# A routed attention kernel whose token lists get slots of 64 B instead of 4 B

## The chip, the core and the metric

The kernel runs on one core of a Trainium2 chip. The metric is the time of the core on the device in microseconds (us): the whole program, from the loads of the inputs to the last row of the output. A profiled execution gives the trace from which the rows below are read.

## What is computed

Three layers follow each other: attention with a window and a few global positions, a layer of eight experts of which each token takes one, and a gated layer.

```python
# attention: batch 4, 8 heads, 768 positions, 64 wide; 8 global positions, window 96
scores = scale * q @ k^T + bias;  scores = where(keep, scores, -1e9)
a = softmax(scores);  attn = a @ v            # x = attn as [3072 tokens, 512]

# experts: 8 experts, 512 -> 1024 -> 512; each token goes to its best one
expert_idx = argmax(x @ w_gate);  gate_w = softmax(...)[expert_idx]
for e in range(8):
    mask = expert_idx == e
    out[mask] = gate_w[mask] * (relu(x[mask] @ w1[e]) @ w2[e])

# gated layer: 512 -> 1536 -> 512
y = (sigmoid(x @ w_gate) * (x @ w_val)) @ w_out
```

## The kernel before

**Attention** (0 to about 225 us) works through 24 tiles of 128 tokens. The order of its steps on each engine is written by a planner in the program (`plan`, with tables of costs and ranks), ahead of any run; on the chip each engine takes its steps in that order and waits where a semaphore is missing. Loads of q, k and v (`load`, L460 and L468) are issued from SyncE's queue (SP) two tiles ahead. The first rows of a sequence's v are copied to a tile `spec` (L617, from ScalarE's queue), and VectorE copies `spec` into later v tiles (L487).

**Routing.** For each tile, the chain of steps X to SC finds each token's expert and its slot in that expert's list: L gives the logits, POS counts with two matmuls how many earlier tokens took the same expert, SI adds this to the start of the expert's region, RR stores the token rows (with the gate weight as column 513) into the DRAM tensor `xd` (L731, SP), and SC (L734, GpSimd, called POOL in the trace) scatters the 128 token ids of the tile into the list `lst` in DRAM. `lst` has a region of 3072 slots for each of the eight experts; the slots of an expert are filled in the order of the tokens. The first scatter waits for the fill of `lst` with the number of an empty row (`clear(0)`, L176, SP), which also fills `ids`.

**Experts** (about 225 to 540 us). `ITEMS` names nine pieces of work, (rank of the expert by load, first slot, number of tokens). For each item `iload` (L970, SP) reads the ids of its slots from `lst` into a tile `idx`, one word into each partition, `gather` (L1015, GpSimd) fetches the token rows of `xd` by `idx`, `xgate`, `xturn`, `xhigh` and `xlow` prepare them, and `mm1` (L1100) and `mm2` (L1117) multiply. `icopy` (L1087, SP) copies the item's part of `lst` behind the others into `ids`, so that `ids` holds all tokens in the order of the expert work. The first item's expert is chosen after 19 tiles (`HEAD`), so its list, its rows and its weights come while attention still runs. The last attention tile, its routing and its scatter (`g.tail`) stand among the first matmuls of the experts. The list of the second item is read after that last scatter. From the third pair of weight tiles on, the split weights go to a pool `keep` (`whigh`, L998, ScalarE; `wlow`, L1003, VectorE), which takes over memory of the attention part, that of the token row tiles among it; so L998 has to wait until the last stores from there into `xd` have landed.

**Gated layer** (about 540 to 1095 us). `Gated` reads the expert outputs `yT` in the order of `ids` and scatters the output rows, 2048 B each, by `idt` (L1474, GpSimd), which L1197 (SP) loads from `ids`, again one word into each partition. This load stands in SP's order ahead of the first loads of `yT` (`yfetch`).

Four fills of zeros into `yT` (L183, SP, 1152 KB each) are spread over the attention part.

Of the kernel before, what the change touches and what calls it, by code (L numbers as in the profile page):

```python
# [11 lines left out]
I32 = mybir.dt.int32  # L12
# [6 lines left out]
NT = B * S  # L19
DM = H * D  # L20
E = 8
# [3 lines left out]
NTILE = NT // 128  # L25
# [2 lines left out]
G0 = 24  # L28
WIN = 256 - G0
REG = 3072  # L30
ROW = DM + 1
BIG = float(2.0 ** 38)
EPS = 1e-9
# [17 lines left out]
YPAD = 640  # L51
# [19 lines left out]
def bc(ap, axis, n):  # L71
    a = ap.unsqueeze(axis)
    shape = list(a.shape)
    shape[axis] = n
    return a.to_broadcast(shape)
# [57 lines left out]
def constants(tc, g, tmp):  # L133
    nc = tc.nc
    c = g.const
    tri = tmp.tile([128, 128], I32, name="tri_i")
    nc.gpsimd.iota(tri, pattern=[[1, 128]], base=0, channel_multiplier=-1)
    g.tri = c.tile([128, 128], F16, name="tri")
    nc.gpsimd.tensor_single_scalar(g.tri, tri, 0.0, op=ALU.is_gt)
    g.ones16 = c.tile([128, 128], F16, name="ones16")  # L140
    nc.gpsimd.memset(g.ones16, 1.0)
    w8 = tmp.tile([128, E], I32, name="w8")
    nc.gpsimd.iota(w8, pattern=[[-1, E]], base=E, channel_multiplier=0)
    g.w8 = c.tile([128, E], F32, name="w8f")
    nc.gpsimd.tensor_copy(g.w8, w8)
    c0 = tmp.tile([128, E], I32, name="c0")
    nc.gpsimd.iota(c0, pattern=[[REG // 128, E]], base=0, channel_multiplier=0)
    g.cum = [c.tile([128, E], F16, name=f"cum{i}") for i in range(4)]
    nc.gpsimd.tensor_copy(g.cum[0], c0)
    g.ebase = c.tile([128, E], F32, name="ebase")  # L150
    nc.gpsimd.tensor_single_scalar(g.ebase, c0, 128.0, op=ALU.mult)
    it8 = tmp.tile([128, E], I32, name="it8")
    nc.gpsimd.iota(it8, pattern=[[1, E]], base=0, channel_multiplier=0)
    g.it8 = c.tile([128, E], F32, name="it8f")
    nc.gpsimd.tensor_copy(g.it8, it8)
    tie = tmp.tile([128, E, E], I32, name="tie")
    nc.gpsimd.iota(tie, pattern=[[1, E], [-1, E]], base=0, channel_multiplier=0)
    g.tie = c.tile([128, E, E], F32, name="tief")
    nc.gpsimd.tensor_scalar(g.tie, tie, 0.0, 0.5, op0=ALU.is_gt, op1=ALU.subtract)
    g.idall = c.tile([128, NTILE], I32, name="idall")  # L160
    nc.gpsimd.iota(g.idall, pattern=[[128, NTILE]], base=0, channel_multiplier=1)
    none = tmp.tile([128, E * REG // 128], I32, name="none")
    nc.gpsimd.memset(none, NT)
    zero = tmp.tile([128, YZ], F32, name="zero")
    nc.gpsimd.memset(zero, 0.0)
    wl = g.wl
    g.wg = c.tile([128, 2, KD, E], F16, name="wg")
    nc.gpsimd.tensor_scalar(g.wg[:, 0], wl, -XSC, 0.0, op0=ALU.mult, op1=ALU.add)
    nc.gpsimd.tensor_scalar(wl, wl, -XSC, 0.0, op0=ALU.mult, op1=ALU.add)
    nc.gpsimd.tensor_tensor(g.wg[:, 1], wl, g.wg[:, 0], op=ALU.subtract)  # L170

    def clear(n):


        if n == 0:
            nc.sync.dma_start(out=g.lst.rearrange("(p n) o -> p (n o)", p=128), in_=none)  # L176
            nc.sync.dma_start(
                out=g.ids.rearrange("(p n) o -> p (n o)", p=128), in_=none[:, 0 : (NT + YPAD) // 128]
            )
            nc.sync.dma_start(out=g.xd[NT].rearrange("(p n) -> p n", p=ROW // 171), in_=zero[: ROW // 171, :171])  # L180
        elif n in ZAT:
            c = YC + ZAT.index(n) * YZ
            nc.sync.dma_start(  # L183
                out=g.yT.rearrange("(k p) n -> p k n", p=128)[:, :, c : c + YZ], in_=bc(zero, 1, KD)
            )

    return clear
# [238 lines left out]
def attention(ctx, tc, g):  # L426
    nc = tc.nc
# [14 lines left out]
    tmp = tmps.enter_context(tc.tile_pool(name="tmp", bufs=1))  # L442
# [290 lines left out]
    def SC(bank, t):  # L733
        nc.gpsimd.indirect_dma_start(  # L734
            out=g.lstv[t],
            out_offset=bass.IndirectOffsetOnAxis(ap=chain.pop(t)["si"], axis=0),
            in_=g.idall[:, t : t + 1],
            in_offset=None,
            bounds_check=E * REG - 1,
            oob_is_err=False,  # L740
        )
        del xr[t]
# [202 lines left out]
class Moe:  # L945
# [20 lines left out]
    def iload(self, i):  # L966
        r, c0, n = ITEMS[i]
        g, m = self.g, -(-n // 128)
        x = self.idx[i] = g.const.tile([128, 4], I32, name=f"idx{i}")
        self.tc.nc.sync.dma_start(  # L970
            out=x[:, 0:m],
            in_=g.lst[bass.ds(g.ereg[r] * REG + c0, 128 * m), :].rearrange("(j p) o -> p (j o)", p=128),
        )

    def wload(self, z, p):
# [83 lines left out]
def ffn(ctx, tc, g):  # L1059
# [79 lines left out]
    for n, (i, f) in enumerate(steps):  # L1139
        p = (n + 1) // 2  # L1140
        px = 3
        if n == 2 * NF:
            kps.close()
        if 0 < i < NIT - 1 and px <= f < px + nj[i + 1]:
            moe.xprep(i + 1, f - px)
        z = f % 2
        w = p + 1 - z
        if NF + 4 <= n < NF + 8:
            moe.wsplit(z, 2 * NP + (n - NF - 4) // 2)
        if 1 < w < 2 * NP or 2 * NP + 1 < w:  # L1150
            moe.wsplit(z, w)
        if NF <= n < 2 * NF - 2:
            moe.wload(z, 2 * NP + (n - NF) // 2)
        for w in (p + 3 - z, p + 2 - z):
            if (2 < w < NP or 2 * NP + 2 < w < PLAST) if w > p + 2 - z else w >= PLAST:
                moe.wload(z, w)
        if 0 < i < NIT - 1 and px - 2 <= f < px - 2 + nj[i + 1]:
            moe.xgate(i + 1, f - px + 2)
        prep.finish()
        if i == NIT - 1 and f > 5:  # L1160
            m2.asplit(0, f - 6)
        if n + 1 < len(steps):
            mm1(*steps[n + 1])
        if n == 0:
            g.tail[2]()
            moe.wlow(1, 1)
        if n == 2:
            routing(tc, g, g.cv.tile([128, 512], F32, tag="scratch", name="scratch"))
        if i == 0 and f in (4, 5):
            moe.xgate(1, f - 4)  # L1170
        if i == 0 and f == 6:
            moe.xprep(1, 0)
            moe.xprep(1, 1)
        if i == 0 and f == 2:
            moe.iload(1)
        if i == 0 and f == 3:
            for j in range(nj[1]):
                moe.gather(1, j)
            icopy(0)
        if i + 2 < NIT:  # L1180
            if f == 4:
                head(i + 2)
                moe.iload(i + 2)
            elif f == 6:
                for j in range(nj[i + 2]):
                    moe.gather(i + 2, j)
        if i + 1 < NIT and f == 5:
            icopy(i + 1)
        if i == 1 and f < 2:
            prep.load()  # L1190
        elif f < PREP[i] + (2 if i == 1 else 0):
            prep.start()
            prep.load()
        if i == NIT - 1:
            if f == 0:
                g.idt = g.const.tile([128, NTILE], I32, name="idt")
                nc.sync.dma_start(out=g.idt, in_=g.ids[0:NT, :].rearrange("(t p) o -> p (t o)", p=128))  # L1197
                cvs.close()
                xa1.close()
                m2 = Gated(tc, g, ctx)  # L1200
            m2.lead(f)
        mm2(i, f)
# [457 lines left out]
def spill(ctx, tc, g):  # L1660
# [50 lines left out]
    with tc.For_i(0, n, 1) as i:  # L1711
        e = nc.values_load(who[0:1, ds(i, 1)], min_val=0, max_val=E - 1)
        s = nc.values_load(at[0:1, ds(i, 1)], min_val=0, max_val=E * REG - 128)
        nc.sync.dma_start(out=idx, in_=g.lst[ds(s, 128), :])
        nc.gpsimd.indirect_dma_start(
            out=x, out_offset=None, in_=g.xd, in_offset=bass.IndirectOffsetOnAxis(ap=idx, axis=0)
        )
        V.tensor_scalar(y, x[:, 0:DM], x[:, DM : DM + 1], None, op0=ALU.mult)
        do.turn(do.xT, y)
        V.tensor_copy(y, do.expert(e))  # L1720
        V.tensor_copy(y, do.gated(y))
        nc.gpsimd.indirect_dma_start(
            out=g.out,
            out_offset=bass.IndirectOffsetOnAxis(ap=idx, axis=0),
            in_=y,
            in_offset=None,
            bounds_check=NT - 1,
            oob_is_err=False,
        )
# [125 lines left out]
def attn_moe_kernel(  # L1855
# [22 lines left out]
    g.ps = ctx.enter_context(tc.tile_pool(name="ps", bufs=1, space=bass.MemoryType.PSUM))  # L1878
    dram = ctx.enter_context(tc.tile_pool(name="dram", bufs=1, space=bass.MemoryType.DRAM))
    g.xd = dram.tile([NT + 1, ROW], F32, name="xd")  # L1880
    g.lst = dram.tile([E * REG, 1], I32, name="lst")
    g.lstv = dram_disjoint_views(g.lst, NTILE)
    g.outv = dram_disjoint_views(g.out, NTILE)
    g.yT = dram.tile([DM, NT + YPAD], F32, name="yT")
    g.up32 = dram.tile([NJ, 2, 2, 128, DM], F32, name="up32")
    g.wc = dram.tile([8, 128, NJ, 256], F32, name="wc")
    g.ids = dram.tile([NT + YPAD, 1], I32, name="ids")
    g.us = [dram.tile([128, 7 * 256], F32, name=f"us{s}") for s in range(NSET)]
    g.wz = [dram.tile([128, 2 * NJ * 256], F32, name=f"wz{n}") for n in range(len(ORDER))]
    with tc.manual_schedule():  # L1890
# [49 lines left out]
```

## Time and profile before

| | |
|---|---|
| three runs | 1099.27 us median, 1092.94 to 1100.37 |
| profiled execution | 1097.69 us, of it a span of 1095.9 us from first to last instruction |
| granted TensorE clock, mean | 0.978 |
| TensorE busy | 1027.4 us, 94% of the span |
| VectorE, ScalarE, GpSimd busy | 77%, 52%, 41% |
| chain that ended last | TensorE 72%, VectorE 11%, DMA 4%, GpSimd 4% |
| DMA | 223.62 MB, mean 204 GB/s |

The busy shares are means over stages that differ. The chain that ended last is followed back from the last instruction: at each step to what released it. In the table of stretches "DMA share" is the mean busy share of the 16 DMA engines; packets count in the stretch in which they begin, so it can pass 1.

### The profile page before, as it was taken

Reading aid. Unit: us, or ns where it says so; the run is one execution under the profiler, and the core shown is the slowest. Engines: PE = TensorE matmul, PEld = TensorE weight load, DVE = VectorE, ACT = ScalarE, POOL = GpSimd, SP = SyncE. Lnnn points to the kernel's source line nnn. Section 1 sums busy time; section 2 is a strip of 40 time slices with the busy share of each in tenths; the row PEclk is TensorE's granted clock in tenths of the full one; section 3 lists DMA queues with packets and bytes.
Section 4 is the critical chain, followed back from the end, with each engine's and each line's share of the span. In section 5 each row is a group of like instructions: output and inputs, shape, how many; then the busy total and the mean of one; then the engine's idle time right before and its main releaser. Section 6 shows DMA issues by size and latency. Waiting matters only on the chain.

```text
span 1095.9 us, 21411 instructions
## 1 busy us (share of the span) xinstructions
PE 1027.4 (94%) x7983; PEld 979.7 (89%) x7983; DVE 841.6 (77%) x1683; ACT 565.4 (52%) x1027; POOL 444.5 (41%) x608
## 2 busy tenths in 40 slices
PE   6979798789999999999899998999999999999994
PEld 4768677589889999999899998999999999999994
DVE  5979888855779878975767699666986669766783
ACT  5979888623344444544544464443544345444440
POOL 7879998841221321130869813224222140222102
PEclk9989999889999999999999999999999999999998
DMA  9469997477798899987568758664365634646061
GB/s 186 100 137 193 154 157 138 94 151 234 239 282 273 275 307 304 300 270 201 190 232 284 270 184 317 231 225 145 136 248 205 239 103 174 248 167 244 34 230 63
DMA packets 167385, 223.62 MB, mean 204 GB/s; under 512 B 89603, under 2 KB 131206, under 8 KB 163686
## 3 DMA queue, kind: packets, MB, share of 16 engines
q1 hardware_dynamic: 161670, 208.14, 63.5%
q0 software_dynamic: 5008, 13.93, 4.1%
q8 instruction: 65, 1.06, 0.4%
q14 instruction: 50, 0.41, 0.2%
q10 hardware_dynamic: 592, 0.08, 0.1%
HBM read 163.13 MB, written 58.94 MB: 203 GB/s over the span
## 4 chain that ended last, share of the span: by engine, by line
PE 72%; DVE 11%; DMA 4%; POOL 4%; issue 3%; ACT 2%; SPq 0%; POOLq 0%; DVEq 0%; ACTq 0%
PE q L1330 30%; PE p L1428 13%; PE hp L1100 12%; PE acc L1117 12%; DVE tt L541 2%; DMA spec<-vv 2%; DVE pl L596 2%; DMA xd<-xr 1%; PE mxt L1035 1%; DMA qn<-in_q_dram 1%; DVE set L1320 1%; PE ptp L570 1%; DVE vv L487 1%; ACT pp L558 1%; DVE xt L658 1%
## 5 line engine op out<-in xcount | busy, mean ns | idle before, releaser
L1330 PE MATMUL q<-yo,set 128*128 128x384 f32 x2016 | 354.1, 337 | 2.6 <-ACT set L1278 1.3
L1330 PEld LDWEIGHTS q<-yo,set 128*128 128x128 f32 x2016 | 348.9, 188 | 6.8 <-DVE h L1384 2.1
L1428 PE MATMUL p<-wy,set 128*128 128x256 f32 x1458 | 175.5, 282 | 5.6 <-DVE set L1320 4.0
L1428 PEld LDWEIGHTS p<-wy,set 128*128 128x128 f32 x1458 | 173.6, 189 | 7.4 <-DVE set L1320 5.3
L1100 PE MATMUL hp<-xT,wh 128*128 128x256 f32 (+7 forms) x576 | 147.2, 340 | 2.5 <-ACT wh L998 2.3
L1388 POOL TENSOR_TENSOR h<-h,t 128x384 f32<-128x384 f32 x60 | 60.5, 1016 | 164.3 <-DVE t L1384 160.7
L1279 DVE TENSOR_TENSOR set<-raw,set 128x1024 fp32r<-128x1024 f32 x96 | 110.2, 1151 | 2.3 <-ACT set L1278 2.3
L1100 PEld LDWEIGHTS hp<-xT,wh 128*128 128x128 f32 x576 | 101.6, 191 | 5.9 <-ACT wh L998 2.9
L1100 PE MATMUL hp<-xT,wl 128*128 128x256 f32 (+7 forms) x288 | 96.8, 336 | 1.3 <-DVE wl L1003 1.3
L1117 PE MATMUL acc<-hl,wh 128*128 128x256 f32 (+7 forms) x288 | 96.4, 335 | 0.5 <-DVE hl L1105 0.4
L1117 PE MATMUL acc<-hh,wh 128*128 128x256 f32 (+7 forms) x288 | 96.5, 335 | 0.0
L1117 PE MATMUL acc<-hh,wl 128*128 128x256 f32 (+7 forms) x288 | 96.2, 334 | 0.0
L1015 POOL DMA_INDIRECT x<-xd,idx x29 | 33.3, 1148 | 153.6 <-DMA idx<-lst 146.9
L1003 DVE TENSOR_TENSOR wl<-wr,wh 128x1024 fp32r<-128x1024 f32 x64 | 82.8, 1295 | 16.1 <-ACT wh L998 15.4
L1278 ACT ACTIVATE set<-raw 128x1024 fp32r<-128x1024 f32 x96 | 85.8, 944 | 16.0 <-PE p L1428 12.6
L1104 ACT ACTIVATE hh<-hp 128x256 fp32r<-128x256 f32 (+7 forms) x72 | 34.6, 481 | 114.3 <-PE hp L1100 114.0
L1351 ACT ACTIVATE u<-q 128x384 f32<-128x384 f32 x48 | 23.6, 491 | 121.9 <-PE q L1330 121.9
L558 ACT ACTIVATE pp<-tt,mall 128x232 f32<-128x232 f32 (+1 forms) x192 | 81.2, 484 | 6.6 <-DVE mall L541 4.2
L1353 DVE TENSOR_TENSOR u<-q,u 128x384 f32<-128x384 f32 x48 | 26.8, 558 | 74.9 <-PE q L1330 74.9
L1474 POOL DMA_INDIRECT out_dram<-o,idt x24 | 25.2, 1050 | 145.6 <-ACT set L1278 77.3
L1319 ACT ACTIVATE set<-h 128x1152 fp32r<-128x1152 f32 (+1 forms) x60 | 62.8, 1098 | 37.4 <-DVE h L1395 16.3
L1320 DVE TENSOR_TENSOR set<-h,set 128x1152 fp32r<-128x1152 f32 (+1 forms) x60 | 76.9, 1319 | 2.0 <-ACT set L1319 1.9
(202 smaller groups left out, 2083.7 us busy)
## 6 DMA issues: line engine op xcount, KB each, us to landing
wr<-in_moe_w_dram SPq DMA_DIRECT2D x64, 512.0 KB, 6.6
raw<-us SPq DMA_DIRECT2D x36, 896.0 KB, 4.7
wy<-wz SPq DMA_DIRECT2D x21, 1536.0 KB, 7.5
us<-raw SPq DMA_DIRECT2D x12, 896.0 KB, 4.4
wz<-wy SPq DMA_DIRECT2D x7, 1536.0 KB, 6.2
kn<-in_k_dram SPq DMA_DIRECT2D x24, 256.0 KB, 7.2
qn<-in_q_dram SPq DMA_DIRECT2D x24, 256.0 KB, 6.3
vn<-in_v_dram SPq DMA_DIRECT2D x24, 256.0 KB, 6.8
```

The lines of the kernel that those rows point to most:

```text
L558: nc.scalar.activation(pp[s][:, j, 256 - w :], tt[s][:, j, :w], AF.Exp, bias=g.mall[:, t, h : h + 1], scale=-1.0)
L1003: self.tc.nc.vector.tensor_tensor(lo, self.raws.pop((z, p)), hi.bitcast(F32), op=ALU.subtract)
L1100: nc.tensor.matmul(bk, a[:, k, fs], b[:, k, :], start=(m == 0), stop=(m == 11))
L1104: nc.scalar.activation(hh, bk, AF.Relu)
L1117: nc.tensor.matmul(acc[i][dk], a[:, f % 2, d], b, start=(f == 0 and m == 0), stop=(f == NF - 1 and m == 2))
L1278: self.tc.nc.scalar.activation(h, x, AF.Copy)
L1279: self.tc.nc.vector.tensor_tensor(l, x, h.bitcast(F32), op=ALU.subtract)
L1319: self.tc.nc.scalar.activation(h, x, AF.Copy)
L1320: self.tc.nc.vector.tensor_tensor(l, x, h.bitcast(F32), op=ALU.subtract)
L1330: nc.tensor.matmul(bk, w[:, za, a, us], self.y[zy][:, y, u, :], start=(start and n == 0), stop=(n == 5), skip_group_check=not start,)
L1388: (V if last else G).tensor_tensor(at(half, tok), at(half, tok), d, op=ALU.mult)
L1428: nc.tensor.matmul(bks[t], w[:, za, j, 128 * t : 128 * t + 128], y[:, zy, j, :], start=(new and j == 0 and m == 0 and (end or t != 1)), st ...
```

## The change

The lists `lst` and `ids` in DRAM get 16 words for each slot (LW = 16, 64 B) instead of one. The tile `idall`, from which the ids are scattered, holds each id 16 times, and the scatter writes all 16 words of a slot. The fill of both lists writes 16 times as much: 1536 KB instead of 96 for `lst`, 232 KB instead of 14.5 for `ids`. The tile `none` from which it is done has four times the words, and four copies of it make up `lst`. Loads of `idx` and `idt` take the first word of each slot. The copies from `lst` to `ids` move whole slots.

No instruction changes its place on any engine. On SP each address into the lists takes one more register operation.

```diff
+LW = 16
...
-    g.idall = c.tile([128, NTILE], I32, name="idall")
-    nc.gpsimd.iota(g.idall, pattern=[[128, NTILE]], base=0, channel_multiplier=1)
-    none = tmp.tile([128, E * REG // 128], I32, name="none")
+    g.idall = c.tile([128, NTILE, LW], I32, name="idall")
+    nc.gpsimd.iota(g.idall, pattern=[[128, NTILE], [0, LW]], base=0, channel_multiplier=1)
+    none = tmp.tile([128, E * REG // 512 * LW], I32, name="none")
     nc.gpsimd.memset(none, NT)
...
-            nc.sync.dma_start(out=g.lst.rearrange("(p n) o -> p (n o)", p=128), in_=none)
+            nc.sync.dma_start(out=g.lst.rearrange("(p a n) o -> p a (n o)", p=128, a=4), in_=bc(none, 1, 4))
             nc.sync.dma_start(
-                out=g.ids.rearrange("(p n) o -> p (n o)", p=128), in_=none[:, 0 : (NT + YPAD) // 128]
+                out=g.ids.rearrange("(p n) o -> p (n o)", p=128), in_=none[:, 0 : (NT + YPAD) // 128 * LW]
             )
...
         nc.gpsimd.indirect_dma_start(
             out=g.lstv[t],
             out_offset=bass.IndirectOffsetOnAxis(ap=chain.pop(t)["si"], axis=0),
-            in_=g.idall[:, t : t + 1],
+            in_=g.idall[:, t, :],
...
             out=x[:, 0:m],
-            in_=g.lst[bass.ds(g.ereg[r] * REG + c0, 128 * m), :].rearrange("(j p) o -> p (j o)", p=128),
+            in_=g.lst[bass.ds(g.ereg[r] * REG + c0, 128 * m), 0:1].rearrange("(j p) o -> p (j o)", p=128),
...
-                nc.sync.dma_start(out=g.idt, in_=g.ids[0:NT, :].rearrange("(t p) o -> p (t o)", p=128))
+                nc.sync.dma_start(out=g.idt, in_=g.ids[0:NT, 0:1].rearrange("(t p) o -> p (t o)", p=128))
...
-    g.lst = dram.tile([E * REG, 1], I32, name="lst")
+    g.lst = dram.tile([E * REG, LW], I32, name="lst")
...
-    g.ids = dram.tile([NT + YPAD, 1], I32, name="ids")
+    g.ids = dram.tile([NT + YPAD, LW], I32, name="ids")
```

## Rows read from the trace of the kernel before

**Rows 1.** The page, busy us, share of the span and instructions:
```profile
PE 1027.4 (94%) x7983; PEld 979.7 (89%) x7983; DVE 841.6 (77%) x1683; ACT 565.4 (52%) x1027; POOL 444.5 (41%) x608
```

**Rows 2.** The tile idall: duration ns min/median/max, first and last start us; landing:
```profile
L734 POOL DMA_INDIRECT lst<-idall,si x24: 993/1060/1742, 40.7 to 228.9; - x24
...
DMA to landing us min/median/max: 4.1/7.7/9.9
```

**Rows 3.** Stretches: length, busy PE, PEld, DVE, ACT, POOL; PEclk, DMA share, GB/s:
```profile
27.00:31.00 4.00, 4.00 (x63) 3.63 (x63) 3.79 (x14) 3.81 (x11) 0.69 (x2) 0.89 1.21 234
65.00:66.00 1.00, 1.00 (x16) 0.81 (x15) 1.00 (x10) 1.00 (x5) 1.00 (x2) 1.00 1.06 301
66.00:71.00 5.00, 4.27 (x62) 3.24 (x56) 3.25 (x15) 4.80 (x14) 4.42 (x14) 1.00 1.09 146
...
188.00:196.00 8.00, 7.66 (x119) 6.56 (x117) 7.15 (x26) 7.66 (x19) 7.05 (x13) 0.98 0.00 0
204.00:208.00 4.00, 2.28 (x26) 1.55 (x24) 3.40 (x12) 3.94 (x10) 3.97 (x6) 1.00 1.07 65
224.00:230.00 6.00, 6.00 (x61) 5.86 (x61) 4.95 (x15) 1.48 (x5) 3.27 (x4) 1.00 1.23 122
230.00:235.00 5.00, 3.96 (x34) 3.72 (x32) 0.42 (x1) 0.04 (x1) 0.94 (x9) 1.00 0.69 86
235.00:240.00 5.00, 3.26 (x13) 2.97 (x14) 3.40 (x12) 2.27 (x3) 0.00 (x0) 0.61 0.37 129
680.00:692.00 12.00, 12.00 (x85) 12.00 (x84) 8.84 (x14) 3.14 (x6) 7.11 (x6) 1.00 0.74 248
```

**Rows 4.** Waits of SyncE's queue, 185 to 200 us: total us, times, longest:
```profile
SPq L970 <- DMA lst<-idall,si: 6.3, 1, 6.3
```

**Rows 5.** GpSimd in order of time, two scatters: start us, us, instruction [idle before]:
```profile
63.44 1.06 POOL L734 DMA_INDIRECT lst<-idall,si  x1 [0.17 <-DVE pl L596]
...
200.51 1.06 POOL L734 DMA_INDIRECT lst<-idall,si  x1 [0.16 <-issue]
```

**Rows 6.** The tile idt, the output scatters: duration ns, first and last start us:
```profile
L1474 POOL DMA_INDIRECT out_dram<-o,idt x24: 966/976/1651, 680.8 to 1083.9; - x24
```

**Rows 7.** VectorE in order of time, three instructions behind DMAs:
```profile
75.40 0.42 DVE L487 COPY vv<-spec 32x1040 f16<-32x1040 f16 x1 [4.74 <-DMA spec<-vv]
...
173.57 0.91 DVE L487 COPY vv<-spec 32x1040 f16<-32x1040 f16 x1 [1.60 <-DMA spec<-vv]
...
245.46 0.49 DVE L1026 TENSOR_SCALAR xg<-x 128x512 f32<-128x512 f32 x1 [0.37 <-DMA x<-xd,idx]
```

**Rows 8.** ScalarE in order of time, the first split into the pool keep:
```profile
235.17 1.06 ACT L998 ACTIVATE wh<-wr 128x1024 fp32r<-128x1024 f32 x1 [5.13 <-DMA xd<-x]
```

**Rows 9.** The chain that ended last, 220 to 245 us: start us, us, what:
```profile
221.45 13.49 DMA xd<-xr
...
237.54 2.50 PE hp L1100 x10
240.04 2.56 PE acc L1117 x12
...
244.21 1.42 PE acc L1117 x12
```

**Rows 10.** DMA issues, 212 to 216.5 us: count, KB each, us to landing:
```profile
xd<-xr SPq DMA_DIRECT2D x2, 256.5 KB, 3.4
```

**Rows 11.** GpSimd in order of time, the second item's first gather:
```profile
241.19 1.76 POOL L1015 DMA_INDIRECT x<-xd,idx  x1 [10.24 <-DMA idx<-lst]
```

**Rows 12.** SyncE's queue in order of time, the fill of lst:
```profile
23.13 1.10 SPq L176 DMA_DIRECT2D lst<-none  x1
```

**Rows 13.** TensorE in order of time, the transposes of tile 6's k:
```profile
45.72 0.60 PE L494 MATMUL tp<-ident,kn 128*128 128x128 f32 x4
```

**Rows 14.** GpSimd in order of time, the start:
```profile
5.54 0.25 POOL L163 MEMSET none<- 128x192 int32 x1
...
7.88 1.40 POOL L126 TENSOR_SCALAR nb<-dd 128x128 f32<-128x128 f32 x4 [0.71 <-DVE dd L118]
```

More of the change, by code (lines that the diff above doesn't have):

```diff
@@ L1713, in spill @@
         s = nc.values_load(at[0:1, ds(i, 1)], min_val=0, max_val=E * REG - 128)
-        nc.sync.dma_start(out=idx, in_=g.lst[ds(s, 128), :])
+        nc.sync.dma_start(out=idx, in_=g.lst[ds(s, 128), 0:1])
         nc.gpsimd.indirect_dma_start(
```

## Prediction

> **What bounds the kernel now.** I read the page first: TensorE is busy for 94% of the span [rows 1], so only what lets it idle, or slows the work that feeds it, can move the end. The lists are written and read in the attention part and at its end (0 to 260 us), so the next view is that of the lists' scatters: 24 of them, from 40.7 to 228.9 us, about 1.06 us each on GpSimd, landing 4.1 to 9.9 us after their start, 7.7 in the median [rows 2]. One scatter carries 128 words, 512 B. The bytes don't explain 7.7 us.
>
> Then the table of stretches, to see what the DMA engines do while a scatter lands. From 188 to 196 us they are idle (share 0.00, 0 GB/s) [rows 3], and in just that time SyncE waits 6.3 us for a scatter's landing [rows 4]. So the landing is not spent in a queue behind other bytes; the memory takes that long to confirm 128 words. In other stretches it costs the neighbours too. I divide GB/s by the busy share, which gives the rate of engines that are busy throughout: 284 GB/s at 65 to 66 us, just after a scatter issued at 63.44 [rows 5], and 134 in the five us that follow; 61 at 204 to 208, behind the scatter issued at 200.51; 99 at 224 to 230 and 125 at 230 to 235, behind the last ones [rows 3]. The output scatters, which move rows of 2048 B and begin at 680.8 [rows 6], leave 335 GB/s at 680 to 692 us [rows 3]. So it is not the scatter as such: **the 4 B pieces hold up the DMA engines for some 5 us each time.**
>
> Last, where anybody waits for that. Three places: VectorE idles 4.74 us until 75.40 and 1.60 us until 173.57 for the copy of the global rows, spec [rows 7]. And ScalarE idles 5.13 us until 235.17 for the last store of token rows into xd [rows 8]; the chain of waits shows the store before it with 13.49 us to its landing [rows 9], and two such stores in a quiet stretch land after 3.4 us [rows 10]. TensorE runs dry behind it: 1.04 us idle in 230 to 235, 1.74 in 235 to 240, and the granted clock is 0.61 in the second [rows 3]. In the chain the matmul groups then take 2.50 us (ten of them) and 2.56, against 1.42 for twelve at 244 us [rows 9].
>
> **The change part by part.** The instructions and their order stay as they are on every engine; shapes change, and SyncE computes a list address with one more register operation.
>
> The scatters. Each of the 128 ids becomes a 64 B piece in a slot of its own. Before, the ids of one tile fall on eight runs of neighbouring words, one run for each expert, so about 16 of them share 64 B; after, none do. GpSimd's 1.06 us is for 128 pieces either way, cost 0. What the memory does with 64 B pieces no row shows. The nearest rows on both sides: 4 B pieces hold (the stretches above), 2048 B pieces do not. Between them lies the fill of the ordered ids, 128 pieces of 116 B, issued right behind that of lst at 23.13 [rows 12]; from 27 to 31 us, soon after it, loads in 256 B pieces run at 193 GB/s of full share [rows 3]. 64 B is nearer to that, so I take "does not hold" as the likeliest and "holds as before" as the other end. The Trainium skill (page DMA: Bandwidth & Descriptors, section Specifications) draws the line elsewhere: below 512 B a DMA reads, modifies and writes, so 64 B pieces would be no better off than 4 B ones. By that sentence the gains below would be zero and the sum the old time; the 116 B fill speaks against it, but it is one small DMA.
>
> What goes if the spells go:
> (a) The spec copy behind the wait until 75.40 queues behind a zero fill of yT and loads. The stretch 66 to 71 moves 0.73 MB; at the 301 GB/s of the us before it that takes 2.4 us, not 5 [rows 3]. Gain 2.6 of the 4.74 us; ends 0 and 4.7.
> (b) The later spec copy: the same share of 1.60 us, 0.9; ends 0 and 1.6.
> (c) The last store of xd. ScalarE's wait ends about when it lands, 235.1. The quiet 3.4 us, against 13.49 for the store before it, would let ScalarE start at its work at once, up to 5.1 us earlier, and TensorE's 1.04 + 1.74 = 2.8 us of idle time go. If the clock then doesn't fall, the slow groups come back as well: 2.50 - 1.18 (ten at the pace of twelve in 1.42) plus 2.56 - 1.42 = 2.5 us. I take 2.8 and two thirds of 2.5, 4.5 us; ends 0 and 5.3.
>
> What is late next at (c): the first gather by the second list starts at 241.19, when its list has landed [rows 11], 12.3 us after the last scatter's start; if that scatter lands in 4.1 us instead of some 9, the gather starts near 236, again 5 us earlier. VectorE waits 0.37 us for its rows now, until 245.46 [rows 7]; it keeps pace, and takes nothing back.
>
> The other spells cost nothing now: the loads of q, k and v are issued two tiles ahead, and no long wait is put down to them. Their going gives nothing.
>
> The fills. lst grows from 96 KB to 1.57 MB and ids from 14.5 to 238 KB, together 1.81 MB in pieces of 3072 and 1856 B, issued from 23.13 on [rows 12]. At 301 GB/s this lasts 6.0 us, at the 146 of a disturbed stretch 12.4; it ends between 30 and 37 us. Two things wait behind it: the first scatter at 40.7 [rows 2] and the k load that follows in SyncE's order, which TensorE transposes at 45.72 [rows 13]. Cost 0, with 4 us to spare at the worse rate. Without that cover each us later is a us on GpSimd.
>
> GpSimd's start. Setting none takes 0.25 us for 192 elements [rows 14]. 576 more there and 360 more in idall cost at most in proportion, 1.2 us; GpSimd idles 0.71 us for VectorE a little later [rows 14], so at most 0.5 is left, and I take 0.3.
>
> The loads of single words. Nine idx loads and idt still move one word per piece, now 64 B apart. Not in the trace; at least nothing, perhaps a little less than now, at most what 256 B pieces cost: idt's 3072 at 234 GB/s take 3.4 us [rows 3], and it stands ahead of yT's first loads in SyncE's order. The number of pieces stays, so I take 0.2 us; ends 0 and 3.4. The copies from lst to ids keep 16 pieces each, 1 to 2 KB instead of 64 to 120 B: 0.
>
> **Sum.** -2.6 - 0.9 - 4.5 + 0.3 + 0.2 = -7.5 us. The profiled execution took 1097.69 us (span 1095.9 and 1.8 around it), so 1090.2; against the median of the three runs, 1099.27, it would be 1091.8. I say 1090.5.
>
> **Rivals.**
> First, 64 B pieces hold the engines as 4 B ones do, and the change doesn't do what it says: a, b and c are zero, +0.5 remains, 1098.2 by the profiled execution, 1099.8 by the median. For it: no row shows a scatter of 64 B. Against it: the 116 B pieces, and the neighbours that no longer share 64 B. This is also the outcome by the page's 512 B.
> Second, the spells go, but each stall is taken over by the next wait. At (a) the copy still queues behind 1.2 MB of zeros; at (c) the clock falls all the same. Then only the 2.8 us of (c) come, 1095.
> Third, slower: the 1.81 MB fill. It decides from 110 GB/s downwards (1.81 MB in the 16.5 us from 24.2, the end of its issue, to 40.7). At the 86 GB/s of 230 to 235 us [rows 3] it would end at 45.3, GpSimd would stand 4.6 us at its first scatter with all its attention work queued behind, and the k load for 45.72 would come late as well: 1097.7 + 4.6 = 1102.3 if the spells stay too. Against it: that rate belongs to a stretch behind scatters, and none has run by then.
>
> **How the numbers follow.** Forecast 0.62, with 1085 to 1094 as its own range (all of a, b and c gives 11.6 us, 1086; the runs differ by 7 us); first rival 0.22, second 0.11, third 0.05. For 8 in 10 the range goes up to the first rival's median and leaves out the third and the tails: 1084 to 1100. This kernel's runs tell a change from none at about 1%, 11 us. The forecast passes that only with all three terms in full, about 1 in 3: faster 0.22, slower 0.04, same 0.74.
>
> **What would show it.** Right: scatters land in 2 to 5 us; the stretches behind them keep over 230 GB/s of full share; VectorE's waits for spec fall from 4.74 and 1.60 below 2.5 and 0.8; ScalarE's 5.13 us and TensorE's dry spell at 230 to 240 are gone; the matmul groups there take 1.4 us. Wrong: landings stay near 7.7 us (first rival); landings fall but the waits stay (second); GpSimd stands before the first scatter (third). If the late stages, bound by TensorE, change by more than 2 us, something outside this account moved.

## The result, and the profile after

The changed kernel takes 1088.55 us in the median of nine runs (1087.47 to 1090.66), the kernel before 1098.76 beside it (1092.94 to 1102.43): a ratio of 0.991, 95% interval 0.9889 to 0.9932. The profiled execution took 1088.45 us, its span 1086.5. So 10 us came off, 7.5 were forecast, and the runs lie closer together than before. The page after, against [rows 1]: TensorE works 3.2 us less, and 9.4 us of span are gone, so most of what went was idle time.

```profile
PE 1024.2 (94%) x7983; PEld 979.4 (90%) x7983; DVE 840.6 (77%) x1683; ACT 564.8 (52%) x1027; POOL 448.6 (41%) x608
```

The scatters next: the view of the tile idall after, which answers to [rows 2].

```profile
L735 POOL DMA_INDIRECT lst<-idall,si x24: 993/1060/1745, 39.2 to 221.0; - x24
...
DMA to landing us min/median/max: 2.8/4.7/6.1
```

GpSimd spends the same 1.06 us on a scatter; the landing takes 4.7 us in the median instead of 7.7. Where SyncE waited 6.3 us for one in a quiet stretch [rows 4], it waits 2.4 now, in the waits of its queue from 176 to 200 us after:

```profile
SPq L971 <- DMA lst<-idall,si: 2.4, 1, 2.4
```

Then the stretches. The changed kernel reaches the end of attention 8 us earlier, so what lay at 204 to 208 and 224 to 240 in [rows 3] now lies at 196 to 200 and 216 to 232, and 65 to 71 at 63 to 69 (columns as there; the last three rows are used below).

```profile
63.10:64.10 1.00, 1.00 (x16) 0.81 (x15) 1.00 (x10) 1.00 (x5) 1.00 (x2) 1.00 1.64 101
64.10:69.10 5.00, 4.29 (x62) 3.26 (x56) 3.59 (x16) 4.82 (x14) 4.42 (x14) 1.00 0.63 131
195.90:199.90 4.00, 2.31 (x27) 1.57 (x25) 3.41 (x12) 3.97 (x10) 3.97 (x6) 1.00 0.43 125
216.10:222.10 6.00, 6.00 (x61) 5.85 (x61) 4.94 (x15) 1.49 (x6) 3.14 (x3) 1.00 0.42 112
222.10:227.10 5.00, 5.00 (x45) 4.96 (x44) 3.56 (x11) 2.35 (x4) 0.93 (x9) 1.00 0.51 176
227.10:232.10 5.00, 5.00 (x45) 5.00 (x43) 4.14 (x12) 2.66 (x4) 3.02 (x2) 1.00 0.24 42
64.00:192.00 128.00, 108.25 (x1719) 92.78 (x1714) 116.11 (x490) 114.59 (x301) 117.41 (x228) 0.99 0.66 156
229.00:242.00 13.00, 12.97 (x110) 12.77 (x109) 7.70 (x14) 4.31 (x9) 6.42 (x6) 1.00 0.46 123
530.00:545.00 15.00, 15.00 (x82) 14.78 (x81) 10.12 (x15) 6.43 (x11) 8.97 (x10) 0.92 0.71 244
```

GB/s by the busy share gives 291 behind the scatter of 192.44 us, where it was 61, and 267 and 345 behind the last ones, where it was 99 and 125; the last five of these us, in which the engines are 0.24 busy, have 175. At 63 to 69 us the rate is 62 in the first us and 208 in the five that follow, where it was 284 and 134: here a slow spell is left, and the runs with longer rows below show where it comes from. TensorE is busy in every one of the 16 us from 216 to 232, at a granted clock of 1.00; before, it idled 2.8 us in the same work and fell to a clock of 0.61.

VectorE in order of time after, against [rows 7]:

```profile
68.76 0.42 DVE L488 COPY vv<-spec 32x1040 f16<-32x1040 f16 x1
...
164.97 0.85 DVE L488 COPY vv<-spec 32x1040 f16<-32x1040 f16 x1
...
233.12 0.49 DVE L1027 TENSOR_SCALAR xg<-x 128x512 f32<-128x512 f32 x1 [1.68 <-DMA x<-xd,idx]
```

No bracket stands behind the two copies any more: the waits of 4.74 and 1.60 us are gone. The third row has a longer wait than before, 1.68 us for gathered rows against 0.37, but comes 12.3 us earlier, and TensorE is busy throughout. ScalarE's first split has no wait either, where [rows 8] had 5.13 us:

```profile
222.05 1.06 ACT L999 ACTIVATE wh<-wr 128x1024 fp32r<-128x1024 f32 x1
```

In the chain of waits the groups of twelve matmuls now go at one pace (rows from 229 us, against [rows 9]); no store of xd with 13.49 us is left in it.

```profile
228.93 1.44 PE hp L1101 x12
230.36 1.42 PE acc L1118 x12
```

GpSimd in order of time, the same gather as [rows 11]. It starts 12.6 us earlier, of which attention brought 7.9 (the last scatter started at 228.88, now at 220.97):

```profile
228.62 1.90 POOL L1016 DMA_INDIRECT x<-xd,idx  x1 [5.58 <-DMA idx<-lst]
```

**Where the time came off**, read from the same instruction in both kernels. GpSimd in order of time, scatters on either side of the two spec copies, before:

```profile
70.93 1.06 POOL L734 DMA_INDIRECT lst<-idall,si  x1 [0.16 <-issue]
...
92.23 1.06 POOL L734 DMA_INDIRECT lst<-idall,si  x1 [0.17 <-issue]
...
171.46 1.06 POOL L734 DMA_INDIRECT lst<-idall,si  x1 [0.28 <-DVE d L629]
184.49 1.05 POOL L734 DMA_INDIRECT lst<-idall,si  x1 [0.32 <-DVE hn L752]
```

and after:

```profile
69.01 1.10 POOL L735 DMA_INDIRECT lst<-idall,si  x1 [0.16 <-issue]
...
85.92 1.06 POOL L735 DMA_INDIRECT lst<-idall,si  x1 [0.17 <-issue]
...
164.54 1.06 POOL L735 DMA_INDIRECT lst<-idall,si  x1 [0.28 <-DVE d L630]
176.40 1.05 POOL L735 DMA_INDIRECT lst<-idall,si  x1 [0.32 <-DVE hn L753]
```

Later landmarks are the nine copies of a list into ids (start of the first and the last), before and after,

```profile
L1087 SPq DMA_DIRECT2D ids<-lst x9: 532/617/705, 238.9 to 497.2; - x9
```

```profile
L1088 SPq DMA_DIRECT2D ids<-lst x9: 536/606/689, 226.6 to 483.6; - x9
```

and the output scatters after, against [rows 6]:

```profile
L1475 POOL DMA_INDIRECT out_dram<-o,idt x24: 967/974/1654, 667.8 to 1074.5; - x24
```

| landmark | before, us | after, us | earlier by |
|---|---|---|---|
| first scatter | 40.67 | 39.18 | 1.5 |
| scatter ahead of the first spec wait | 70.93 | 69.01 | 1.9 |
| scatter behind it | 92.23 | 85.92 | 6.3 |
| scatter ahead of the second | 171.46 | 164.54 | 6.9 |
| scatter behind it | 184.49 | 176.40 | 8.1 |
| last scatter | 228.88 | 220.97 | 7.9 |
| last copy into ids | 497.2 | 483.6 | 13.6 |
| first output scatter | 680.8 | 667.8 | 13.0 |
| last output scatter | 1083.9 | 1074.5 | 9.4 |
| span | 1095.9 | 1086.5 | 9.4 |

The three places of the forecast gave 4.4, 1.2 and 5.7 us; another 2.3 came off the start and the stretches between, and 4.2 were lost again after 484 us.

### The profile page after: what moved, and what is told of

Same layout as the page of the kernel before. It is cut to its first block, busy times and chain, and to the rows that moved or that the text cites. A ratio compares the mean times of both kernels' runs of the same rounds, so it can differ in the third digit from the quotient of the medians.

```text
span 1086.5 us, 21412 instructions
## 1 busy us (share of the span) xinstructions
PE 1024.2 (94%) x7983; PEld 979.4 (90%) x7983; DVE 840.6 (77%) x1683; ACT 564.8 (52%) x1027; POOL 448.6 (41%) x608
## 3 DMA queue, kind: packets, MB, share of 16 engines
q8 instruction: 65, 1.06, 0.4%
## 4 chain that ended last, share of the span: by engine, by line
PE 71%; DVE 12%; POOL 6%; issue 3%; ACT 2%; DMA 2%; SPq 0%; ACTq 0%; POOLq 0%; DVEq 0%
PE q L1331 31%; PE p L1429 14%; PE acc L1118 12%; PE hp L1101 12%; DVE tt L542 2%; DVE pl L597 2%; PE mxt L1036 1%; DVE xt L659 1%; DVE vv L488 1%; ACT pp L559 1%; POOL xr L640 1%; DVE set L1321 1%; DVE h L1313 1%; DVE kT L509 1%; POOL raw L1240 1%
## 5 line engine op out<-in xcount | busy, mean ns | idle before, releaser
L1429 PEld LDWEIGHTS p<-wy,set 128*128 128x128 f32 x1458 | 175.8, 191 | 6.2 <-DVE set L1321 4.7
L1279 ACT ACTIVATE set<-raw 128x1024 fp32r<-128x1024 f32 x96 | 85.8, 945 | 16.4 <-PE p L1429 13.0
```

Source lines behind the costliest of these rows:

```text
L1279: self.tc.nc.scalar.activation(h, x, AF.Copy)
L1429: nc.tensor.matmul(bks[t], w[:, za, j, 128 * t : 128 * t + 128], y[:, zy, j, :], start=(new and j == 0 and m == 0 and (end or t != 1)), st ...
```

## The experiments

Two theories stand against each other. **Neighbours:** pieces that fall into the same 64 B hold the DMA engines; what counts is the spacing. **Small pieces:** a piece under some size holds an engine wherever it falls; what counts is the size. A third, that the gain has nothing to do with the pieces (addresses, another start), needs a control. The kernel before ran beside each group, 15 to 23 times, and its median moves by 7 us from group to group, so ratios are compared; the others ran 6 to 12 times.

| kernel | us | before beside it | ratio, 95% interval |
|---|---|---|---|
| e1_gap4 | 1093.19 | 1104.78 | 0.9899, 0.9878 to 0.9919 |
| e2_slot16 | 1096.38 | 1104.78 | 0.9935, 0.9909 to 0.9961 |
| e3_slot128 | 1095.69 | 1104.78 | 0.9926, 0.9907 to 0.9945 |
| e4_fill | 1106.96 | 1104.78 | 1.0027, 1.0011 to 1.0043 |
| e5_listonly | 1098.35 | 1097.34 | 1.0013, 0.9996 to 1.0031 |
| e6_noscatter | 1089.81 | 1097.34 | 0.9936, 0.9911 to 0.9961 |
| e7_row2112 | 1085.59 | 1097.34 | 0.9897, 0.9873 to 0.9921 |
| e8_row2112_4B | 1095.79 | 1097.34 | 0.9987, 0.9968 to 1.0006 |
| e9_copyword | 1092.02 | 1100.72 | 0.9915, 0.9896 to 0.9934 |
| e10_change | 1092.46 | 1100.72 | 0.9921, 0.9900 to 0.9942 |
| e11_row2112 | 1089.78 | 1100.72 | 0.9896, 0.9877 to 0.9915 |
| e12_lastoff | 1096.92 | 1100.72 | 0.9961, 0.9942 to 0.9980 |

**e1_gap4: the spacing without the size.** On top of the change:

```
-    nc.vector.tensor_tensor(c["sl"], lg.pop(t)[:, E : 2 * E], c["oh"], op=ALU.mult)
+    nc.vector.scalar_tensor_tensor(c["sl"], lg.pop(t)[:, E : 2 * E], float(LW), c["oh"], ...)
...
-        in_=g.idall[:, t, :],
+        in_=g.idall[:, t, 0:1],
...
-    g.lst = dram.tile([E * REG, LW], I32, name="lst")
+    lst = dram.tile([E * REG * LW, 1], I32, name="lst")   # scattered into by word, read by slot
```

> Lists of ids in slots 64 B apart as in the change, but each scatter writes only the one 4 B word of a slot. Theory of the neighbours (pieces that fall into the same 64 B hold the DMA engines): the spacing is what cures, so the time is that of the change, 1088 to 1091 us, the scatters land in about 4.7 us, and the stretch 64:192 has a DMA share near 0.66 at 156 GB/s. Theory of the small piece (a piece under some size holds an engine wherever it falls): as before the change, 1096 to 1101 us, landings near 7.7 us, a share near 0.93 at about 160 GB/s. A time between, with landings between, would say that both count.

The ratio is that of the change. The stretch 64 to 192 us of this kernel:

```profile
64.00:192.00 128.00, 108.41 (x1700) 92.60 (x1697) 115.72 (x495) 115.19 (x302) 117.53 (x228) 0.99 0.70 157
```

A share of 0.70 at 157 GB/s, against 0.66 at 156 for the change. The trace also has the time of each DMA packet. Between 40 and 240 us 330 packets of SyncE's and GpSimd's DMAs took over 1 us in the kernel before, 4 in the change and 7 here. Pieces of 4 B do no harm when each has 64 B to itself: the small-piece theory falls. (The landings are not in this trace.)

**e2_slot16 and e3_slot128: other slots.** One line, `LW = 4` and `LW = 32`.

> Slots and pieces of 16 B, with everything else as in the change. Theory of the neighbours: four slots still share 64 B, so part of the hold stays: 1092 to 1098 us, landings of 5.5 to 7.5 us, a DMA share of 0.75 to 0.9 in 64:192. Theory of the small piece: not cured, 1096 to 1101 us. If the gain had nothing to do with the slots' size but only with pieces of more than one word, 1088 to 1091 us.

> Slots and pieces of 128 B, the fill of the list doubled to 3.1 MB. Theory of the neighbours: 64 B is already alone in its block, so no further gain: landings near 4.7 us, share near 0.66 in 64:192, and 1088 to 1092 us, with up to some 4 us more if the longer fill delays the loads of the first 40 us. Theory of the small piece: the larger piece cures more, landings under 4.5 us and a share under 0.63, 1085 to 1088 us.

By their times the two can't be told apart, and the change itself did not run in this group; e1_gap4 beside them has 0.9899. The traces tell more. With 16 B the hold is partly back: 102 packets of over 1 us, the longest of 5.0. The waits of ScalarE, 200 to 262 us, of that kernel (total us, times, longest) show where it costs: the stall at the end of attention is there again, now put down to a load.

```profile
ACT wh L999 <- DMA wr<-in_moe_w_dram: 5.4, 1, 5.4
```

With 128 B nothing more is won; the ratio's interval overlaps that of the change, and if anything the kernel is slower. It has 67 packets of over 1 us, none above 1.6; the largest group, some 30 of them at 102 to 106 us, stands behind two stores of token rows and ahead of the next scatter's own pieces. Slots of 32 B were not tried: the block that must not be shared is larger than 16 B and at most 64 B, and the text writes 64 B for it. The share in 64 to 192 us was 0.77 for 16 B and 0.78 for 128 B, so here it told less than I expected of it: four kernels with 4 B slots had shares of 0.75, 0.76, 0.85 and 0.93 there (e12_lastoff, e8_row2112_4B, e4_fill, the kernel before). What stalls somebody tells the cases apart, the mean share does not.

**e4_fill: the control for addresses and bytes.** On the kernel before:

```
-    nc.sync.dma_start(out=g.lst.rearrange("(p n) o -> p (n o)", p=128), in_=none)
+    nc.sync.dma_start(out=g.lst.rearrange(...), in_=none); nc.sync.dma_start(out=g.pad.rearrange("(p a n) o -> p a (n o)", p=128, a=15), in_=bc(none, 1, 15))
...
+    g.pad = dram.tile([E * REG * 15, 1], I32, name="pad")   # right behind lst
```

> The kernel before, with a second list behind the first that nothing reads: it is filled in the same place with the other 15/16 of the bytes that the change fills, and every later tensor in HBM lies as far on as in the change. The scatters stay 4 B. If the gain came from addresses or from another start, 1088 to 1092 us. Theories of the pieces: as before, 1096 to 1102 us, with the price of the fill on top, which I put at 0 to 1 us; landings near 7.7 us and a share near 0.93 in 64:192.

No gain: a loss of 0.11 to 0.43% by the interval, 1 to 5 us, with 249 packets of over 1 us. The third theory falls, for `lst` and the tensors that follow it (`ids` keeps its 4 B slots here). That the loss is the fill's is not shown: the stalls stay at the old places, VectorE's waits for spec among them. Its waits of 20 to 262 us, before, after, in e1_gap4 and in e4_fill (total us, times, longest):

```profile
DVE vv L487 <- DMA spec<-vv: 9.1, 3, 4.7
```

```profile
DVE vv L488 <- DMA spec<-vv: 1.7, 1, 1.7
```

```profile
DVE vv L488 <- DMA spec<-vv: 2.5, 2, 2.2
```

```profile
DVE vv L488 <- DMA spec<-vv: 10.7, 4, 4.0
```

**e12_lastoff: the largest term alone.** On the kernel before:

```
-            bounds_check=E * REG - 1,
+            bounds_check=E * REG - 1 if t < NTILE - 4 else 0,
```

> The kernel before, 4 B slots and all, with only the scatters of the last four tiles kept from writing by their bound: they are issued as before, and the last 512 tokens stay out of the lists, which is left out of the output too. It tries the largest term of the sum alone, the stores of xd and the first gathers held behind these four scatters from 217 to 241 us. Theory of the neighbours with that term: 4 to 6 us gained, ratio 0.994 to 0.997, the wait of ScalarE of 5.13 us until 235.17 gone, the two others of VectorE still there. If the held engines cost little there and the gain is spread over the whole attention part: 0 to 2 us, ratio 0.998 to 1.001.

0.9961 is 4.3 us. The tile ids and the scatters of that kernel:

```profile
L1088 SPq DMA_DIRECT2D ids<-lst x9: 533/618/705, 233.8 to 491.1; - x9
```

```profile
L735 POOL DMA_INDIRECT lst<-idall,si x24: 993/1061/1742, 40.2 to 228.3; - x24
```

At the last scatter it is 0.6 us ahead of the kernel before, at the last copy 6.1: 5.5 us come off between, which is what the change takes off there (13.6 - 7.9 = 5.7). VectorE's first spec wait is still there:

```profile
75.24 0.42 DVE L488 COPY vv<-spec 32x1040 f16<-32x1040 f16 x1 [5.07 <-DMA spec<-vv]
```

ScalarE's wait for the stores of xd is gone, and from 220 to 240 us no packet of SyncE's or GpSimd's DMAs takes over 1 us. By the trace, four scatters that write nothing give the term in full; by the ratio it is 2.2 to 6.4 us. (Tokens that are in no list also let the gathers behind read the zero row more often; what that does was not separated.)

**e6_noscatter: the floor.** On the change:

```
-            bounds_check=E * REG - 1,
+            bounds_check=0,
...
+    lists = tmp.tile(...); nc.gpsimd.iota(lists, ...)   # every token in order; fills lst for each expert
...
-    ap=self.g.idt[:, n : n + 1]
+    ap=self.g.idt[:, n, 0:1]                            # g.idt = g.idall: the tokens' own order
```

> The change with the scatters issued as before but kept from writing (their bound lets only slot 0 through), the lists filled from the start with every token in order, and the output rows written in the tokens' own order: it leaves out the routing, so the output is not the reference's, but every load, gather and matmul stays. It gives the floor. Theory of the neighbours, with 64 B as the full cure: the scatters of the change hold nothing, so the same time as the change, ratio 0.988 to 0.993, share 0.64 to 0.67 in 64:192. If scatters of 64 B still hold the engines (the rest that I see near 63, 128 and 141 us of the changed kernel), a share of 0.60 or less and 1.5 to 4 us faster than the change, ratio 0.986 to 0.988.

Scatters that write nothing land hardly sooner than those of the change (4.7 us in the median); those of e7_row2112 below, with 64 B slots, land after 3.7, so this is no lower bound:

```profile
L735 POOL DMA_INDIRECT lst<-idall,si x24: 994/1059/1742, 41.9 to 222.2; - x24
...
DMA to landing us min/median/max: 2.7/4.6/8.0
```

The kernel as a whole is no faster than the change (0.9936 against 0.991 to 0.9921; neither range that I had set was met, and the share in 64 to 192 us is 0.68). Its first scatter starts at 41.9 us instead of 39.2; that the lists that it has to make are the reason was not tried. From the first scatter to the last it takes 180.3 us; the change took 181.8, and e5_listonly, with the scatters of the change, 180.6 (40.5 to 221.1). So 0.3 to 1.5 us are left to win in them.

**e5_listonly and e9_copyword: the ordered ids.** In e5_listonly ids keep 4 B and the copy packs them; in e9_copyword both have slots of 64 B and the copy moves one word of each:

```
-    out=g.ids[ds(g.oreg[r] + c0, n), :], in_=g.lst[ds(g.ereg[r] * REG + c0, n), :]
+    out=g.ids[ds(g.oreg[r] + c0, n), :], in_=g.lst[ds(g.ereg[r] * REG + c0, n), 0:1]      # e5, ids [n, 1]
+    out=g.ids[ds(g.oreg[r] + c0, n), 0:1], in_=g.lst[ds(g.ereg[r] * REG + c0, n), 0:1]    # e9, ids [n, 16]
```

> The change for the token lists alone: the ordered ids keep their slots of 4 B, and the copy of a list into them picks one word of each 64 B slot. Theory of the neighbours: all of the gain comes from the scatters into the lists, so the ratio to the kernel before is that of the change, 0.988 to 0.993, and DMA share in 64:192 near 0.66; the copies now write words into one 64 B block, after 480 us, where the queues have time, 0 to 1 us. If the ordered ids have a part of the gain, the ratio is 0.995 or more.

> The change, with slots of 64 B for the lists and for the ordered ids, but the copies of the lists into the ordered ids move one 4 B word of each slot, as many pieces as in the run with the lists alone (up to 480 in a copy), each now into a 64 B block of its own. Theory of the neighbours: the copies land in 3 to 6.5 us as in the change (with the lists alone 6.7 to 12.3), the gathers of rows behind them in about 4 us, and the ratio to the kernel before is that of the change, 0.988 to 0.993. If the number of small pieces is what held the queues there: copies of 8 us and more, gathers at 229 us of 10 us and more, ratio 0.997 to 1.003.

The first of these I got wrong: the whole gain was gone. I had placed the copies after 480 us, but two of them are issued at 226.8 and 230.1, in the most sensitive place. The tile ids, the chain of waits, and the stretch behind them in e5_listonly:

```profile
L1088 SPq DMA_DIRECT2D ids<-lst x9: 538/608/692, 226.8 to 495.3; - x9
...
DMA to landing us min/median/max: 6.7/9.8/12.3
```

```profile
228.77 13.15 DMA x<-xd,idx
```

```profile
229.00:242.00 13.00, 7.22 (x61) 7.01 (x59) 2.63 (x5) 2.11 (x5) 4.66 (x4) 0.95 0.81 61
```

Attention kept its gain (the last scatter starts at 221.1 us, as in the change), then the copies hold the engines: 0.81 busy for 61 GB/s, a gather of rows lands after 13.15 us, and TensorE works 7.22 of 13 us; 35 packets of the gathers take over 1 us in 230 to 240. It is the fault of before, from another queue and another kind of DMA. The same number of 4 B words, each into 64 B of its own, does no harm; e9_copyword in the same stretch:

```profile
229.00:242.00 13.00, 12.96 (x110) 12.75 (x109) 7.72 (x14) 4.30 (x9) 5.50 (x6) 1.00 0.45 122
```

TensorE's busy time is that of the change within 0.01 us, no packet takes over 1 us between 40 and 240 us, and the ratio is that of the change (0.9915 against 0.9921 beside it). (The landings of these copies are not in the trace.) So the neighbours decide for direct DMAs too.

**e7_row2112, e8_row2112_4B, e10_change, e11_row2112: the rows of xd.** Rows of 2052 B share 64 B with the next row as well.

```
-ROW = DM + 1
+ROW = DM + 16
...
-    nc.vector.reciprocal(xr[t][:, DM : DM + 1], chain[t]["ep"])
+    nc.vector.reciprocal(xr[t][:, DM:ROW].rearrange("p (a b) -> p a b", a=1), bc(chain[t]["ep"], 2, 16))
```

> The change, and the rows of xd made 2112 B long (33 whole blocks of 64 B) instead of 2052 B; the 15 added words hold the scale again. Theory of the neighbours carried on: rows of 2052 B share a 64 B block with the next row, which another engine writes, so the rest of the hold goes too: share 0.62 or less in 64:192 and a ratio of 0.986 to 0.989. If row edges hold nothing, as the change, 0.989 to 0.993, with up to 0.5 us for 3% more bytes in the stores and gathers of xd.

> The kernel before with slots of 4 B, and the rows of xd 2112 B long. If the edges of the rows are the larger part of what holds the engines, ratio 0.990 to 0.995 and a share of 0.75 or less in 64:192. If the 4 B scatters are, as I think, no change: ratio 0.997 to 1.003, share 0.85 to 0.95.

> The change once more, unaltered, so that it stands on the same chip as the run with longer rows. Both theories: ratio 0.988 to 0.993, DMA share 0.64 to 0.68 in 64:192.

> The change with rows of xd of 2112 B once more, beside the change on the same chip. If row edges that share a 64 B block cost time on top of what they cost in DMA share (0.63 against 0.66), 1 to 2.5 us less than the change; if that share lies beside other work, within 1 us of it.

On the kernel before, longer rows alone bring nothing that can be told from no change, though the share (0.76) lies below what I had set for that case and 187 packets of over 1 us are left of 330. On the change they bring 2.7 us beside it on one chip (1089.78, 1088.99 to 1090.63, against 1092.46, 1090.51 to 1094.51); the ratios to the kernel before, 0.9896 and 0.9921, have intervals that overlap. One microsecond shows what is left in the changed kernel, e10_change and then e11_row2112. It stands behind a store of token rows; the pieces of the scatter that started at 62.31 us come later, after 65 us:

```profile
64.00:65.00 1.00, 1.00 (x14) 0.67 (x13) 1.00 (x9) 1.00 (x5) 1.00 (x2) 1.00 1.37 116
```

```profile
64.00:65.00 1.00, 1.00 (x14) 0.68 (x12) 1.00 (x8) 1.00 (x4) 0.92 (x2) 1.00 1.16 218
```

85 GB/s of full share against 188. In 64 to 192 us the shares are 0.66 and 0.62 at 156 GB/s each, and no packet between 40 and 240 us takes over 1 us in either kernel with longer rows on the change. Rows of 2112 B still follow each other without a gap, which speaks for the shared block and against the short distance. Which DMA engine writes a row, and whether `xd` starts on a block of 64 B, the traces do not show. It is the fastest version here.

## Why the prediction was right

- **The mechanism.** "The 4 B pieces hold up the DMA engines for some 5 us each time" holds, with one word changed by e1_gap4, e5_listonly and e9_copyword: it is 4 B pieces that share 64 B. The prediction had named the eight runs of neighbouring words, some 16 ids to 64 B, but weighed sizes between 4 and 2048 B, and its row for that, the 116 B fill, was the wrong scale to ask: from 4 to 128 B the size does not matter here.
- **The landing.** "The memory takes that long to confirm 128 words" is not borne out: scatters that write nothing land after 4.6 us in the median (e6_noscatter), so at most some 3 of the 7.7 us belong to the words.
- **The first rival** falls: 64 B pieces are cured (0.991), 4 B pieces with 64 B each are cured (0.9899), 128 B win nothing more (0.9926). The Trainium skill (DMA: Bandwidth & Descriptors, Specifications) has a DMA below 512 B read, modify and write; these runs do not show whether one does, but the gain does not come at that line.
- **(a)** was taken at 2.6 of 4.74 us, since the copy would still queue behind 0.73 MB; the scatters on either side moved by 4.4, and the whole wait is gone. Too small by 1.8.
- **(b)** 0.9 forecast, 1.2 measured.
- **(c)** 4.5 forecast with ends 0 and 5.3; 5.7 measured, and 5.5 in e12_lastoff where only the last four scatters were changed. The clock did not fall in the groups behind it, so nearly all of the second part came, not two thirds. The gather that was to start near 236 us starts at 228.6, which with the 7.9 us of attention is 236.5 on the old scale.
- **"Their going gives nothing"**, of the other spells: 0.6 us between the two copies. Small, and not zero.
- **The start** was to cost 0.3 us for GpSimd; the first scatter starts 1.5 us earlier instead. Executions differ by as much: e10_change, the same program, is 0.8 us behind it at the fourth scatter (62.31 against 61.53), and e7_row2112, with the same fill of the lists, has its first at 40.6 us. The fill costs nothing that shows here, as forecast, and the single-word loads of idx neither (2.6 us from the list's issue at 226.00 to the gather, 2.9 before).
- **The second rival**, stalls taken over by the next wait, is right only for the 1.68 us of VectorE, which TensorE does not feel; the third, a slow fill, fails at its condition.
- **The late stages** were to move by less than 2 us, or something outside the account moved. It did: 4.2 us are lost again after 484 us. The forecast's 1090.5 against 1088.55 is so the sum of places that each gave more (11.3 us instead of 8.0, and 2.3 elsewhere) and a loss that it didn't have: that the total came out so near is in part luck.

Of that loss 0.6 us is gone by the first output scatter, and 3.6 go between the first and the last. Two things show. The granted clock is 0.92 in 530 to 545 us after, and 1.00 in the same work before:

```profile
540.00:560.00 20.00, 19.33 (x110) 18.85 (x111) 13.00 (x20) 8.94 (x15) 12.06 (x15) 1.00 0.70 231
```

But the lead is 13.0 us again at the first output scatter, so this explains 0.6 us at most. And the matmuls of the gated layer in 950 to 1040 us take 339 ns in the median instead of 336; before, then after:

```profile
L1330 PE MATMUL q<-yo,set x504: 333/336/341, 949.7 to 1036.9; 128*128 128x384 f32 x168
```

```profile
L1331 PE MATMUL q<-yo,set x439: 335/339/342, 949.7 to 1027.1; 128*128 128x384 f32 x147
```

All nine executions with idall of 1.5 or 3 KB a partition (after, e1, e3, e5 to e7, e9 to e11) have 339 or 340 there, all five with 96 or 384 B (before, e2, e4, e8, e12) have 336. Instruction by instruction, the work that TensorE does from 950 to 1036 us in the kernel before takes 85.8 us in each of the five and 87.4 in each of the nine: 1.6 us. What in the wider tile does it, such as where later buffers come to lie, was not tried. The rest of the 4.2 us is open.

## What to carry to other kernels

When DMAs write small pieces, ask how many of them fall into the same 64 B, and not only how small they are: slots of 64 B, or words 64 B apart, took away stalls that looked like slow loads, slow copies and a slow clock elsewhere. Look for it where busy DMA engines move few bytes (GB/s by busy share), then price it only where somebody waits, since most such stretches cost nothing. Widen every link of such a chain together: the list alone, with packed ids behind it, gained nothing.

## What the runs showed of the hardware

- 4 B pieces into a block that other pieces share: 61 to 134 GB/s of full share in the 4 to 6 us behind a scatter [rows 3], and 330 packets of over 1 us between 40 and 240 us. The same pieces 64 B apart: 7 such packets (e1_gap4). Behind packed copies a gather lands after 13.15 us (e5_listonly). Why a shared block holds up the packets behind it, the runs do not show.
- Scatters that write nothing land after 4.6 us in the median, those of 64 B slots after 4.7 (3.7 where the rows beside them are 2112 B long), those of packed words after 7.7.
- The edges of rows of 2052 B do the same on a smaller scale: 85 GB/s of full share in a microsecond behind a store of such rows, 188 with rows of 2112 B.
- TensorE's matmuls of one form have two durations at the same granted clock of 1.00, 336 and 339 ns; the change and the longer rows, profiled twice each, showed the same one both times.
